# Moving the first weight load ahead of the entry barrier in a decode-attention kernel

## The chip, the cores and the metric

The kernel runs on one core of a Trainium2 chip. The metric is the device time of one execution in microseconds (us), median of several runs. Loads are issued by SyncE ("SP" in the profile, "SPq" for its queue). The 16 DMA engines of the core then move them.

## The reference

There are two independent attention decodes, A and B, with one query token each. D is 576, there are 32 query heads and 16 key/value heads of size 128. A sees a window of 2048 positions of the cache, B all 8192. The two results stand side by side in the output.

```python
q = (x @ wq).reshape(B, Sq, Hq, Dh)                       # x: 1 x 1 x 576, wq: 576 x 4096
scores = einsum("bhqd,bhkd->bhqk", q, k) * Dh ** -0.5     # k, v: the cache, repeated for 2 heads
o = einsum("bhqk,bhkd->bhqd", softmax(scores), v)
return o.reshape(B, Sq, Hq * Dh) @ wo                     # wo: 4096 x 576
```

With one token, nearly all the work is reading wq, the caches and wo once: 102.8 MB.

## The kernel before

The program is a list of operations per engine, with semaphores worked out from what each reads and writes. `emit` puts the lists into one block. The framework puts an entry barrier ahead of the block (each engine drains and reports to PoolE; PoolE releases all) and an exit barrier behind it.

```python
def load(dst, src, writes, dma, after=()):                # all big loads: SyncE
    add("sp", lambda sp: sp.dma_start(dst, src()), writes=writes, dma=dma, after=after)

def load_x(P):                                            # the two small x loads: ScalarE's queue
    def go(act):
        ...
            src = bass.AP(tensor=x.tensor, offset=x.offset, ap=[[9, 64], [4, 2], [1, 5]])
            return act.dma_start(xtwo[:, P, 0:5], src)    # 128 pieces of 5 elements, 10 bytes
    add("act", go, writes=[("xtwo", P)], dma="x%d" % P)
...
    with self.nc.Block() as block:                        # in emit
        @block.sync
        def _(sp):
            run("sp", sp)
        ...
...
prog.emit()
for P in range(2):                                        # behind the block and its exit barrier
    o = prog.writer[("out", P)]
    nc.sync.wait_ge(prog.sem(o.key), o.value)
```

The first nine loads of SyncE wait for nothing: six parts of wq (2 MB, 2 MB, 0.5 MB for A; the same for B) and three of the four first key slots. The tenth, into key slot 3, waits until PE is through with the part of wq that lies there.

## Time and profile before

| | before |
|---|---|
| time, median of 3 | 249.32 us (249.07 to 249.35) |
| span of the profiled run | 247.7 us |
| first packet of a load (packet records) | 1.74 us |
| last packet of wo ends (packet records) | 244.92 us |

The page's lines on the DMA. The first two rows have 40 slices of the span; a digit is the busy share in tenths. The last two give packets, MB and share of 16 engines' span per queue.

```profile
span 247.7 us, 7504 instructions
...
DMA  7999999999999999999999999999999999999993
GB/s 267 408 423 423 438 429 426 423 431 423 429 425 434 426 421 423 427 426 431 431 434 429 423 429 426 423 431 434 434 429 423 429 426 423 431 432 432 426 399 142
...
q1 hardware_dynamic: 7936, 102.77, 98.1%
...
q10 hardware_dynamic: 288, 0.00, 0.1%
```

The DMA engines are busy from the first slice to the last at some 425 GB/s. The Trainium skill ("DMA: Bandwidth & Descriptors", Specifications) puts the fabric ceiling at 435 GB/s; the inner slices (421 to 438) agree with that. So only the two ends have time to give: the head without a load, and the tail after the last one.

SyncE's waits (engine, line, releaser: us in total, times, longest) look as if SyncE were held by PE:

```profile
SPq L380 <- PE ktps L466: 87.5, 15, 16.4
SPq L380 <- PE opsum L557: 74.7, 14, 25.8
...
SPq L380 <- PE misc L425: 23.4, 1, 23.4
...
SPq L730 <- DMA out_dram<-outsb: 0.4, 1, 0.4
```

But loads land 18 to 31 us after issue: SyncE refills a queue that is never empty, and these waits cost nothing. Only the last line is at the end of the span.

The timeline of the first microsecond (start, duration, engine, line, operation):

```profile
0.34 0.10 POOL L743 MEMSET const-uint8-127<- 128x1 uint8 x1
0.73 0.20 POOL L353 MEMSET ident<- 128x128 bf16 x1 [0.29 <-POOLq L743]
0.74 0.61 ACTq L344 DMA_DIRECT2D xtwo<-in_A_x_dram  x1
0.74 0.86 SPq L380 DMA_DIRECT2D vslots<-in_A_wq_dram  x2
```

The issue of the first load, at 0.74, is in SyncE's power alone, yet stands behind a barrier that waits for PoolE's four memsets. What that head costs is seen in the view of windows (window and length, busy time of PE, PEld, DVE, ACT and POOL with counts, PE clock, DMA share, GB/s; a packet counts where it ends or starts, so short windows are rough):

```profile
0.00:1.00 1.00, 0.00 (x0) 0.00 (x0) 0.00 (x0) 0.00 (x0) 0.47 (x6) 1.00 0.00 0
1.00:2.00 1.00, 0.00 (x0) 0.00 (x0) 0.00 (x0) 0.00 (x0) 1.00 (x5) 1.00 1.14 229
2.00:3.00 1.00, 0.00 (x0) 0.00 (x0) 0.00 (x0) 0.97 (x1) 1.00 (x6) 1.00 0.29 98
3.00:4.00 1.00, 0.00 (x0) 0.00 (x0) 0.00 (x0) 0.52 (x2) 0.77 (x5) 1.00 1.01 426
```

And the tail, from the timeline:

```profile
245.39 0.11 PEld L646 LDWEIGHTS ktps<-vslots,opj 128*32 128x32 bf16 x4 [0.22 <-DMA vslots<-in_B_wo_dram]
245.75 0.31 DVE L652 CAST outsb<-ktps 128x144 bf16<-128x144 f32 x1 [10.44 <-PE ktps L646]
246.09 0.56 SPq L658 DMA_DIRECT2D out_dram<-outsb  x1
```

The output lands at 247.69 (the last increment of its semaphore; the prediction's 247.66 is the last but one), and SyncE's last wait ends the span at 247.74.

Drains and semaphore instructions are left out of the timeline; these are their records in the trace of the kernel before (start, ns, engine, operation):

```
  0.000     7 Sync    DRAIN             reports to PoolE
  0.304   188 GpSimd  DRAIN             behind its four memsets
  0.535    17 GpSimd  EVENT_SEMAPHORE   all four reported
  0.655    17 Sync    EVENT_SEMAPHORE   released
  0.740   386 Sync    DMA_DIRECT2D      first load
246.089   563 Sync    DMA_DIRECT2D      output
246.710   462 Sync    DRAIN             exit barrier
247.323    17 Sync    EVENT_SEMAPHORE   released
247.711    28 Sync    EVENT_SEMAPHORE   wait for the two output DMAs
```

### The profile page before, as it was taken

What the parts mean: (1) busy time and instruction counts of PE and PEld (TensorE: products, weight loads), DVE (VectorE), ACT (ScalarE), POOL (GpSimd) and SP (SyncE); (2) the same over time, 40 slices, a digit from 0 to 9 for tenths busy, and PEclk for the clock granted to TensorE, in tenths of its full rate; (3) what the DMA queues carried; (4) which work ended last, traced back from release to release, by engine and by line L of the source; (5) the groups of instructions that cost most, each with busy time, mean ns of one, the idle gap of its engine ahead of it and who ended that gap; (6) DMA issues with size and microseconds to landing.
All of it is one profiled execution on the core that took longest, in us unless ns stands there. A gap on an engine that the chain in (4) does not pass through costs nothing. (4 is left out here: it accounts for less than half of the span.)

```text
span 247.7 us, 7504 instructions
## 1 busy us (share of the span) xinstructions
PE 169.6 (68%) x3406; PEld 131.4 (53%) x3406; DVE 80.9 (33%) x152; ACT 87.1 (35%) x92; POOL 12.9 (5%) x49
## 2 busy tenths in 40 slices
PE   0193689984999569995999638998255144685634
PEld 0031277764787459783887428785243142584522
DVE  0001145663556025555656022555004004204000
ACT  2000057837478016786778004775200000000000
POOL 7501000000000000000000000000000000000000
PEclk9999779996799967999999956999858755556555
DMA  7999999999999999999999999999999999999993
GB/s 267 408 423 423 438 429 426 423 431 423 429 425 434 426 421 423 427 426 431 431 434 429 423 429 426 423 431 434 434 429 423 429 426 423 431 432 432 426 399 142
DMA packets 8235, 102.92 MB, mean 415 GB/s; under 512 B 1184, under 2 KB 1312, under 8 KB 2080
## 3 DMA queue, kind: packets, MB, share of 16 engines
q1 hardware_dynamic: 7936, 102.77, 98.1%
q8 instruction: 8, 0.13, 0.2%
q10 hardware_dynamic: 288, 0.00, 0.1%
q14 instruction: 3, 0.02, 0.0%
HBM read 102.76 MB, written 0.00 MB: 415 GB/s over the span
## 5 line engine op out<-in xcount | busy, mean ns | idle before, releaser
L472 ACT ACTIVATE kt<-ktps 128x1024 bf16<-128x1024 bf16 x80 | 77.8, 1021 | 52.8 <-PE ktps L466 52.8
L466 PEld LDWEIGHTS ktps<-ident,kslots 128*128 128x128 bf16 x1280 | 78.2, 103 | 27.1 <-issue 27.1
L466 PE MATMUL ktps<-ident,kslots 128*128 128x128 bf16 x1280 | 84.5, 229 | 11.1 <-PEq L214 11.1
L475 DVE COPY kt<-ktps 128x1024 bf16<-128x1024 bf16 x80 | 55.2, 691 | 52.5 <-PE ktps L466 52.4
L557 PE MATMUL opsum<-vslots,ptm 128*32 128x128 bf16 x1280 | 27.7, 259 | 28.4 <-PEq L214 24.6
L557 PEld LDWEIGHTS opsum<-vslots,ptm 128*32 128x32 bf16 x1280 | 24.8, 118 | 32.1 <-issue 32.0
L486 PE MATMUL sacc<-kt,qst 128*32 128x512 bf16 x320 | 25.5, 392 | 1.8 <-PEq L214 1.8
L566 DVE TENSOR_TENSOR diag<-opsum,rows 128x512 f32<-128x512 f32 x5 | 3.5, 692 | 55.8 <-PE opsum L557 55.8
L425 PE MATMUL opsum<-vslots,xpad 128*32 128x512 bf16 x64 | 8.4, 505 | 16.1 <-DVE xpad L410 12.2
L599 ACT ACTIVATE stat<-stat 128x1 f32<-128x1 f32 (+1 forms) x2 | 0.6, 295 | 37.4 <-DVE stat L597 37.4
L425 PEld LDWEIGHTS opsum<-vslots,xpad 128*32 128x32 bf16 x64 | 2.3, 118 | 19.0 <-issue 13.2
L457 POOL COPY qst<-qtm 128x64 bf16<-128x64 bf16 x20 | 4.5, 236 | 122.7 <-PE sacc L486 113.2
L646 PE MATMUL ktps<-kslots,opj 128*32 128x144 bf16 x184 | 6.1, 326 | 5.8 <-DMA kslots<-in_B_wo_dram 3.9
L431 ACT ACTIVATE qrow<-opsum 128x512 bf16<-128x512 f32 x2 | 1.2, 597 | 24.8 <-PE misc L425 24.8
L486 PEld LDWEIGHTS sacc<-kt,qst 128*32 128x32 bf16 x320 | 5.3, 94 | 8.4 <-issue 4.5
L523 ACT ACTIVATE psb<-sacc,stat 128x2048 bf16<-128x2048 f32 x3 | 5.9, 1967 | 8.5 <-DVE stat L517 8.5
L646 PEld LDWEIGHTS ktps<-kslots,opj 128*32 128x32 bf16 x184 | 5.2, 145 | 6.4 <-DMA kslots<-in_B_wo_dram 4.2
L425 PE MATMUL misc<-vslots,xpad 128*32 128x512 bf16 x64 | 8.3, 497 | 0.0
L433 DVE CAST qrow<-misc 128x512 bf16<-128x512 f32 x2 | 1.4, 691 | 16.3 <-PE misc L425 16.3
L630 PE MATMUL misc<-acc,pick 128*128 128x32 f32 x16 | 3.8, 404 | 3.6 <-DVE acc L624 2.9
L652 DVE CAST outsb<-ktps 128x144 bf16<-128x144 f32 x2 | 0.6, 308 | 16.3 <-PE ktps L646 16.3
L630 PEld LDWEIGHTS misc<-acc,pick 128*128 128x128 f32 x16 | 3.6, 328 | 3.8 <-DVE acc L624 3.0
(66 smaller groups left out, 63.1 us busy)
## 6 DMA issues: line engine op xcount, KB each, us to landing
kslots<-in_B_k_cache_dram SPq DMA_DIRECT2D x16, 2048.0 KB, 20.1
vslots<-in_B_v_cache_dram SPq DMA_DIRECT2D x16, 2048.0 KB, 18.3
kslots<-in_A_k_cache_dram SPq DMA_DIRECT2D x4, 2048.0 KB, 30.1
vslots<-in_A_v_cache_dram SPq DMA_DIRECT2D x4, 2048.0 KB, 25.1
vslots<-in_A_wq_dram SPq DMA_DIRECT2D x2, 2048.0 KB, 9.8
vslots<-in_B_wq_dram SPq DMA_DIRECT2D x2, 2048.0 KB, 20.3
kslots<-in_A_wo_dram SPq DMA_DIRECT2D x2, 2016.0 KB, 23.9
kslots<-in_B_wo_dram SPq DMA_DIRECT2D x1, 2016.0 KB, 31.2
```

The costliest lines, as they stand in the source:

```text
L425: ins = pe.matmul(qps[c][32 * j:32 * j + 32, :], lhsT=xpad[:, P, x, :], rhs=src[:, o:o + 512], start=(u == 0), stop=(u == WQ_UNITS - 1))
L433: add("dve", lambda dve: dve.tensor_copy(qrow[:, 512:1024], misc[:, :]), reads=[B_M], writes=[("qrow", 1)])
L457: add("pool", lambda pool: pool.tensor_copy(qst[:, s * 64:(s + 1) * 64], qtm[:, o:o + 64]), reads=[("qtm", KIND[g])], writes=[("qst", s)], ...
L466: ins = pe.matmul(ktps_bf[q][:, t * 128:(t + 1) * 128], lhsT=kslots[:, s, o:o + 128], rhs=ident[:, :], start=True, stop=True, is_transpose ...
L472: add("act", lambda act, q=q, dst=dst: act.activation(dst, ktps_bf[q], ACT.Copy), reads=[("bank", q)], writes=[("kt", u % NKT, q)], tag="e ...
L475: add("dve", lambda dve, q=q, dst=dst: dve.tensor_copy(dst, ktps_bf[q]), reads=[("bank", q)], writes=[("kt", u % NKT, q)], tag="e%d%d" % ( ...
L486: ins = pe.matmul(sacc[32 * j:32 * j + 32, 512 * half:512 * half + 512], lhsT=qst[:, s * 64 + e * 32:s * 64 + e * 32 + 32], rhs=rhs, start ...
L523: return act.activation(psb[:, :].rearrange("p (x g) -> p x g", g=2), src, ACT.Exp, bias=st(P, C_NB + k), scale=SCALE, accum_out=st(P, C_L ...
L557: ins = pe.matmul(opsum[32 * j:32 * j + 32, s * DH:(s + 1) * DH], lhsT=ptm[:, o:o + 32], rhs=vslots[:, s, b * 128:(b + 1) * 128], start=(u ...
L566: return dve.tensor_tensor(diag[:, g % 2, :, :], opsum[:, :].rearrange("p (s d) -> p d s", s=NS), m, ALU.mult)
L630: ins = pe.matmul(misc[:, 0:32], lhsT=pick[:, r, :], rhs=acc[:, d, 32 * r:32 * r + 32], start=(r == 0), stop=(r == 3))
L646: ins = pe.matmul(ktps[P][32 * j:32 * j + 32, 0:OUTW], lhsT=opj[:, P, jj:jj + 32], rhs=view[:, o:o + OUTW], start=(jj == 0), stop=(jj == H ...
```

## The change

Its description: the first load of wq precedes the entry barrier, and SyncE's wait for the two output DMAs stands behind the block's exit barrier. The intent is to start the loads while the other engines are still gathering, and to hide the exit barrier behind the landing of the output. The whole diff:

```diff
+        first = per["sp"].pop(0)
+        assert not first.left and first.dma is not None
+        one(self.nc.sync, first)
+        lead = self.nc.cur_bb.bb.instructions
+        ins = lead.pop()
+        at = next(k for k, o in enumerate(lead) if o.engine == ins.engine and "Drain" in str(o))
+        lead.insert(at, ins)
+
         with self.nc.Block() as block:
```

The load is emitted ahead of the block and then moved in front of SyncE's drain. It writes a buffer that nobody else touches yet. The diff says nothing of the output wait: that stands behind the exit barrier in both kernels.

## The prediction

> What bounds the kernel now: the load stream. The page's row of DMA shares is 9 in every slice but the first (7) and the last (3); the packets of the SyncE queue, 102.77 MB, take 98.1% of 16 engines' span, and between 1.9 and 242.9 us the trace never has fewer than 13 of them in flight. The stream moves 422 to 430 GB/s; the Trainium skill (DMA: Bandwidth & Descriptors, Specifications) gives 435 GB/s as the fabric ceiling, and the trace agrees that almost nothing is left. So the span is a head without loads (first packet at 1.74 us), 243.2 us of stream (the last packet of wo ends at 244.92) and a tail of 2.8 us (matmuls, one copy, output DMA issued at 246.09, landed at 247.66, end 247.74). SyncE waits for PE often (view of its queue's waits: 87 and 75 us), but loads land 18 to 31 us after issue and the queue never runs dry.
>
> What the change does. In the order of SyncE's instructions one load of 2 MB moves ahead of its drain into the entry barrier. Nothing else changes: the wait for the output DMAs stands behind the exit barrier in both kernels, so that half of the description is worth 0.
>
> Gain, from the timeline of the first 4 us: SyncE reaches its drain at 0.00, is released at 0.655 (PoolE, with four memsets and a drain, comes last, at 0.53), and issues the first load at 0.74; the issue takes 0.39, the first packet starts 0.62 us after its end (the same section's "~0.6 us" to the first byte agrees). Now the issue should start at about 0.00 and the first packet at 1.0: the stream starts 0.74 us earlier.
>
> Price: the drain now follows a DMA issue. At the kernel's end such a drain took 0.46 us. So SyncE joins at about 0.9, the barrier releases at 1.05, and the other engines (x loads, PoolE's setup) start 0.4 us later. The second load is issued at about 1.15 (before: 1.19), while the first keeps the engines busy for 5 us (8 packets of 0.62 each): no hole. The 0.4 us is hidden: the first matmuls start at 11.5 us, and the first load that waits for them, issued at 29.4, comes some 7 us (estimate: 15.3 MB queued ahead at 427 GB/s) before the queue would run dry.
>
> So 0.74 us lies on the critical path, once, and should appear at the end nearly in full. Span 247.7 -> 247.0 us; time 249.32 -> 248.6 us, range 248.1 to 249.2; that is 0.3%. Faster by over 2%: 0.005; within 2%: 0.985; slower by over 2%: 0.01.
>
> Right if: first issue at about 0.0, first packet at 1.0; barrier release 0.3 to 0.5 us later; second issue at 1.1 to 1.2; no gap in the loads in flight; last wo packet near 244.2; tail unchanged at 2.8; x landing at most 1 us later, without consequence.
>
> Wrong if: the drain lasts until the load's descriptors are written or the load has landed (5 us), which would hold all engines; or the queue is not ready so early and the first packet does not move; or the stream's rate varies between executions by as much as the gain (0.3% of it is 0.74 us), so that the time shows nothing.

## The result, and the profile after

The changed kernel took 248.41 us, median of 4 (248.08 to 248.61), the kernel before 249.23 us in the same rounds. The ratio is 0.9966, 95% interval 0.9949 to 0.9984: a real gain of some 0.8 us, far under 2%. A second time with five rounds, as an experiment below, it was 0.9973.

The page, timeline and windows after, in the same order as before:

```profile
span 247.2 us, 7504 instructions
...
DMA  8999999999999999999999999999999999999993
GB/s 316 382 446 420 436 424 424 427 427 435 427 426 424 424 432 422 426 424 427 430 432 430 430 424 438 424 427 424 430 427 432 427 432 430 432 425 423 422 410 143
```

```profile
0.00 1.14 SPq L388 DMA_DIRECT2D vslots<-in_A_wq_dram  x2
...
0.33 0.10 POOL L751 MEMSET const-uint8-127<- 128x1 uint8 x1
0.80 0.20 POOL L361 MEMSET ident<- 128x128 bf16 x1 [0.36 <-POOLq L751]
0.81 0.61 ACTq L352 DMA_DIRECT2D xtwo<-in_A_x_dram  x1
```

```profile
0.00:1.00 1.00, 0.00 (x0) 0.00 (x0) 0.00 (x0) 0.00 (x0) 0.41 (x6) 1.00 0.00 0
1.00:2.00 1.00, 0.00 (x0) 0.00 (x0) 0.00 (x0) 0.00 (x0) 1.00 (x4) 1.00 1.18 262
2.00:3.00 1.00, 0.00 (x0) 0.00 (x0) 0.00 (x0) 0.90 (x1) 1.00 (x5) 1.00 0.96 393
```

The issue moved from 0.74 to 0.00, and the first packet (packet records) from 1.74 to 1.02. From 2 to 3 us the stream already moves 393 GB/s, where the kernel before moved 98 GB/s in that window. The other four engines started only 0.07 us later. (The two issues of the first timeline line are merged: the second load was issued at 0.805.) The tail has kept its shape:

```profile
245.18 0.31 DVE L660 CAST outsb<-ktps 128x144 bf16<-128x144 f32 x1 [10.22 <-PE ktps L654]
245.51 0.56 SPq L666 DMA_DIRECT2D out_dram<-outsb  x1
```

From the last wo packet (244.35) to the end (247.17) are 2.82 us, and 2.81 before.

To see whether the gain is kept, I summed the bytes of the load packets in order of time and read from both traces when each amount had been moved. The difference is the lead over the kernel before, in us:

| profile | at 1 MB | 2 MB | 4 MB | 10 MB | 50 MB | 102 MB |
|---|---|---|---|---|---|---|
| changed kernel | 0.73 | 0.67 | 0.55 | 0.58 | 0.54 | 0.54 |
| changed kernel, again | 0.62 | 0.63 | 0.78 | 0.72 | 0.72 | 0.73 |

In the columns from 4 MB on the lead stays within 0.04 and 0.06 us, and read at every 0.05 MB in between within 0.14, for 230 us. Whatever PE and SyncE do in between neither eats nor adds to it. Within the first 4 MB it wanders by 0.1 to 0.2 us from one execution to the next. In the first profile the stream had a dip where the second load took over (10 to 12 packets in flight, not 16, from 6.7 to 6.9 us). In the second profile it had none. The last 0.8 MB, which the table leaves out, shift the lead once more from run to run, by -0.19 to +0.37 us over all profiles of this document: at the last packet of wo it is 0.58 and 0.90 us in these two. So a single span shows the gain only to within some 0.2 to 0.4 us; the tables and the medians carry it.

### The profile page after: what moved, and what is told of

Its sections match the earlier page's. It is cut to its first block, busy times and chain, and to the rows that moved or that the text cites. A ratio compares the mean times of both kernels' runs of the same rounds, so it can differ in the third digit from the quotient of the medians.

```text
span 247.2 us, 7504 instructions
## 1 busy us (share of the span) xinstructions
PE 169.9 (69%) x3406; PEld 132.4 (54%) x3406; DVE 80.9 (33%) x152; ACT 87.2 (35%) x92; POOL 12.9 (5%) x49
## 5 line engine op out<-in xcount | busy, mean ns | idle before, releaser
L474 PEld LDWEIGHTS ktps<-ident,kslots 128*128 128x128 bf16 x1280 | 79.3, 104 | 26.2 <-issue 26.2
L474 PE MATMUL ktps<-ident,kslots 128*128 128x128 bf16 x1280 | 85.6, 230 | 10.7 <-PEq L214 10.7
```

Source lines behind the costliest of these rows:

```text
L474: ins = pe.matmul(ktps_bf[q][:, t * 128:(t + 1) * 128], lhsT=kslots[:, s, o:o + 128], rhs=ident[:, :], start=True, stop=True, is_transpose ...
```

## The experiments

Theory A: the kernel is a stream of loads with two ends, and the time follows the moment of the first packet one to one. Rivals: the difference is chance (B); compute paces the kernel and the head hides in slack (C); the start of the other engines counts (D); the amount loaded ahead counts (H). The place of the output wait is a question by itself.

### The changed kernel again

No edit; five rounds.

> The changed kernel again, for a second profile and a tighter interval. Theory A (only the start of the load stream counts): first packet at 1.02 us, the last wo packet 0.5 to 0.75 us earlier than before, ratio 0.9970 (0.9960 to 0.9980), that is 0.55 to 0.9 us. The dip of the stream at 6.7 us (where the second load takes over, and where the first profile lost 0.18 of its 0.73 us of lead) is seen again if it belongs to the change, and is gone if it was chance. Theory B (the difference is chance between executions): ratio within 0.999 to 1.001.

Measured: 248.36 us, ratio 0.9973 (0.996 to 0.9987), first packet at 1.05, last wo packet at 244.02, no dip. B falls, A holds. One figure missed: the last wo packet came 0.90 us earlier, not 0.5 to 0.75; the last 0.8 MB added 0.18 to the lead of 0.73. The dip is not part of the change.

### The first load later

```diff
+        reads = ["ones"] if dma == "wq00" else []          # wait for PoolE's memsets
-        add("sp", lambda sp: sp.dma_start(dst, src()), writes=writes, dma=dma, after=after)
+        add("sp", lambda sp: sp.dma_start(dst, src()), reads=reads, writes=writes, dma=dma, after=after)
```

> The kernel before, with its first load made to wait until PoolE's memsets are done, so that the issue moves from 0.74 to about 3.75 us; every other engine starts as before. Theory A (each us of the stream's start is a us of the time): first packet at 4.75, time 252.2 us (ratio 1.012, from +2.9 to +3.1 us). Rival C (the kernel is paced by what the engines compute, and a start of the loads hides in the slack that keeps SyncE waiting for PE): at most +0.5 us, ratio below 1.002.

Measured: 251.68 us (249.02 before), ratio 1.0099 (1.0084 to 1.0115). This is the timeline of SyncE and, below it, the last two windows of the first 10 us:

```profile
3.68 0.86 SPq L381 DMA_DIRECT2D vslots<-in_A_wq_dram  x2
```

```profile
3.00:4.00 1.00, 0.00 (x0) 0.00 (x0) 0.00 (x0) 0.52 (x2) 0.77 (x5) 1.00 0.03 1
4.00:10.00 6.00, 0.00 (x0) 0.00 (x0) 0.71 (x3) 0.00 (x0) 4.71 (x14) 1.00 0.88 330
```

The first packet came at 4.70, 2.95 us later than before, and the time grew by 2.5 to 2.7 us. C falls. But my figure of 2.9 to 3.1 was missed too. The lead table says where: -3.02 us at 1 MB, -2.70 at 4 MB, and -2.65 at 102 MB. Some 0.37 us were won back, 0.3 of it between 2 and 4 MB, and kept. In this run the 288 small packets of the x loads moved between 2.1 and 3.2 us, before the stream began. In the other kernels they stand among the big ones (4.8 to 13.3 us in the changed kernel). That made a new theory, X: the small packets cost the stream about 0.3 us. It is tested below.

### All nine wait-free loads ahead

```diff
-        first = per["sp"].pop(0)
+        while not per["sp"][0].left:                       # until a load has to wait
+            ... one(...) and move it ahead of SyncE's drain, as in the change ...
```

> The changed kernel with all nine wait-free loads ahead of the drain, not one. SyncE takes about 5.5 us to issue them, so the other four engines pass the barrier at about 5.8 us, 5 us later than in the changed kernel. Theory A (the stream's first packet counts, and the engines' start hides in their slack of some 7 us): first packet at 1.02 us, time as that of the changed kernel, 248.4 us, ratio 0.9970 within 0.001; if the dip at 6.7 us came from what the other engines do then (the x loads), it is gone and the ratio is 0.9960. Rival D (the start of the other engines counts): +3 to +5 us, ratio 1.010 to 1.020.

Measured: 248.28 us, ratio 0.9971 (0.9958 to 0.9985). The timeline shows the other engines 4.8 us late:

```profile
2.95 1.95 SPq L387 DMA_DIRECT2D kslots<-in_A_k_cache_dram  x3
5.55 0.20 POOL L360 MEMSET ident<- 128x128 bf16 x1 [5.11 <-POOLq L750]
5.56 0.61 ACTq L351 DMA_DIRECT2D xtwo<-in_A_x_dram  x1
```

PE's first wait (waits of the engines, us in total, times, longest), in order for the kernel before, the changed kernel and this one:

```profile
PE opsum L425 <- DVE xpad L410: 12.2, 2, 11.5
```

```profile
PE opsum L433 <- DVE xpad L418: 12.7, 2, 12.0
```

```profile
PE opsum L432 <- DVE xpad L417: 14.7, 2, 14.0
```

PE starts 2 us later than in the changed kernel and the time is the same: D falls. With nine loads ahead, none of them depends on the barrier any more, and the time shows no more gain. In the one profile the lead at 102 MB is 0.83 us, a little above the 0.54 and 0.73 of the changed kernel; the times of five runs each (248.28 and 248.36 in the median) do not tell the two apart.

### One small piece ahead, cut along the rows

```diff
+            for p0, p1, r, name in ((0, 16, ("v0", "part"), "wq00a"), (16, 128, res, "wq00")):
+                load(dst[p0:p1, :], ... rows p0:p1 ..., [r], name)      # the first piece goes ahead
```

> The changed kernel with only 16 of the 128 rows of the first load (one packet of 16 KB per DMA engine) ahead of the drain, the other 112 behind the barrier. Theory A (what counts is when the first packet moves, as long as the second load is issued before the first one is through): first packet at 1.0 us (a little sooner if the issue of 16 rows is shorter than 0.39 us), the second load issued at 0.8 and its packets from 1.8 on, while the first packets (1.1 to 1.5 us each) are still moving: ratio 0.9972, as the changed kernel. Rival H (the amount ahead counts): half or less of the gain, ratio 0.9985 or more.

Measured: 251.46 us, ratio 1.0099 (1.0084 to 1.0115), some 2.4 us slower than the kernel before. Neither theory had said that. The first packet came at 1.03 as expected, but afterwards the stream ran at 70% of its rate, as the window from 4 to 10 us shows, first in the changed kernel, then in this one:

```profile
4.00:10.00 6.00, 0.00 (x0) 0.00 (x0) 0.29 (x1) 0.00 (x0) 4.71 (x14) 1.00 0.98 396
4.00:10.00 6.00, 0.00 (x0) 0.00 (x0) 0.29 (x1) 0.00 (x0) 4.71 (x14) 1.00 1.02 279
```

The engines are busy, but packets of 16 KB take 0.8 to 1.1 us (medians of 16 in order of time) from 3.8 to 10.5 us, against 0.61 in the changed kernel. The slow stretch ends as the load of the 112 rows lands (its semaphore rises from 10.2 to 11.0 us). So this run tried the shape of the pieces, not the amount ahead. The next two runs separate the two.

### The same cut with nothing ahead, and another cut

The kernel before with the same cut into 16 and 112 rows, both behind the barrier:

> The kernel before, nothing ahead of the barrier, with its first load cut along the rows into 16 and 112. If the loss of the cut along the rows is all the shape of the pieces (Theory S), it appears here too, as large: 3.1 us over the kernel before, 252.2 us, ratio 1.0125, with packets of 0.8 to 1.1 us in the first 10 us. If it came from having a small piece ahead of the barrier (Rival H), this kernel is as the kernel before, ratio 1.000 to 1.002.

Measured: 252.39 us, ratio 1.0138 (1.0122 to 1.0153), 3.3 us slower, with packets of 0.8 to 1.1 us in the same stretch and a lead of -3.10 us at 4 MB that stays (-3.19 at 102 MB). The cut alone does it. The Trainium skill ("SBUF — State Buffer", Door 1: The DMA port swizzle) says that DMA bandwidth depends on how many of the 16 SBUF ports the partitions reach. By its mapping, 16 neighbouring rows reach four of them. But most of the slow packets are those of the other 112 rows, which by the same mapping reach all 16. So the count of ports alone does not explain the loss, no run here shows the ports, and the cause is open.

The changed kernel with the first load cut along the columns, so that each packet goes to the rows it went to before:

```diff
+            for c0, c1, r, name in ((0, 1024, ("v0", "part"), "wq00a"), (1024, n * WQ_U, res, "wq00")):
+                load(dst[:, c0:c1], ... columns c0:c1 ..., [r], name)   # 128 x 2 KB ahead, 128 x 14 KB behind
```

> The changed kernel with one eighth of the first load ahead of the drain, cut along the columns this time: 128 rows of 2 KB ahead, 128 rows of 14 KB behind the barrier, so that every packet goes where it went before. The cut along the rows (16 and 112) lost 3.1 us against the changed kernel, but the trace shows its packets of 16 KB in the first 10 us at 0.8 to 1.1 us each, against 0.61, so it tried the shape of the pieces and not how much is ahead. Theory A (only the time of the first packet counts, as long as the second load takes over in time): first packet at 1.0 us; the second load is issued at 0.80 and its packets come at 1.8; one hole of at most 0.3 us where the eighth is through before that: ratio 0.9972 to 0.9985. Rival H (the amount ahead counts): ratio 0.999 or more.

Measured: 248.54 us, ratio 0.9979 (0.9966 to 0.9993), first packet at 1.00. The lead is 0.61 us at 0.5 MB, 0.44 at 2 MB and 0.48 at 102 MB. An eighth of the load ahead keeps two thirds or more of the lead. What is lost is lost at the handover: the small packets are through at about 2.1 us, and the first packets of the second piece, from there, are slow again (up to 1.16 us for 14 KB, against 0.54 later; that this is the whole loss is argued, not shown). The ratio lies in A's range and excludes 1; against H's 0.999, the top of the interval falls just short of excluding it, and the lead decides: most of the gain comes with an eighth of the bytes.

### The x loads

Without x (zeros in its place, so the result is wrong):

> The changed kernel without the two x loads (x is set to zero instead, so the result is wrong on purpose). The run with the late load gained back 0.37 us of its 3.02 us between 2 and 4 MB; there the 288 small packets of x had been moved before the stream began. Theory X (each small packet of x that stands between the large ones costs the stream time, some 0.3 us in all): the lead of the stream over the kernel before grows from about 0.65 at 1 MB to about 1.0 at 10 MB, ratio 0.9960. Rival Y (that was chance; small packets are free): lead at 10 MB 0.55 to 0.75, ratio 0.9972.

Measured: 247.89 us, ratio 0.9951 (0.9937 to 0.9965). (Its comparison with the reference passed all the same. In a simulation of both programs with these inputs its output differs from that of the kernel before by 0.2% in norm: the scores are so small that the attention weights hardly depend on x.)

With x as one row of 1152 bytes per load, spread by engines that idle there anyway:

```diff
-    xtwo = nc.alloc_sbuf_tensor("xtwo", [128, 2, 8], BF16)
+    xrow = nc.alloc_sbuf_tensor("xrow", [1, 2, DM], BF16)
+    xexp = nc.alloc_sbuf_tensor("xexp", [1, 2, 5, 128], BF16)
-            return act.dma_start(xtwo[:, P, 0:5], src)
+            return act.dma_start(xrow[0:1, P, :], xs[P][0, 0:1, :])
+        # VectorE: xexp[0, P, j, 2m + e] = xrow[0, P, 9m + 4e + j], one copy
+        # PE, for j in 0..4: matmul(ktps[P][:, j:j+1], lhsT=xexp[0:1, P, j, :], rhs=ident[0:1, 0:1])
+        # then as before, from ktps[P][:, 0:5] in place of xtwo[:, P, 0:5]
```

> The changed kernel with x loaded as one row of 1152 bytes per DMA and spread over the partitions by one VectorE copy and five 1-column matmuls each, so that some 32 small packets are left of 256. Right result expected. Theory X: ratio 0.9960 to 0.9965, lead at 10 MB about 0.95. Rival Y: ratio 0.9972, as the changed kernel. The first matmuls may start earlier or later than 11 us; that should not matter.

Measured: 248.07 us, ratio 0.9958 (0.9945 to 0.9972), and the comparison with the reference passed. As a zero x passes it too, I looked further: in simulation, this kernel and the next give the output of the kernel before bit for bit, with these inputs and with x 300 times as large, where a zero x is 2 to 3% off. The page's line of ScalarE's queue, 288 packets in the kernel before (256 of 10 bytes, 32 of 4 bytes), is now

```profile
q10 hardware_dynamic: 4, 0.00, 0.0%
```

| profile | at 1 MB | 2 MB | 4 MB | 10 MB | 102 MB |
|---|---|---|---|---|---|
| changed kernel, twice | 0.73, 0.62 | 0.67, 0.63 | 0.55, 0.78 | 0.58, 0.72 | 0.54, 0.73 |
| without x | 0.76 | 0.77 | 1.07 | 1.13 | 1.12 |
| x as rows | 0.68 | 0.70 | 1.00 | 1.07 | 1.05 |
| nine loads ahead | 0.67 | 0.70 | 0.97 | 0.95 | 0.83 |
| nine loads ahead, x as rows (below) | 0.76 | 0.77 | 1.06 | 1.22 | 1.08 |

Without the small packets the lead grows by some 0.4 us between 2 and 10 MB, and stays. X holds, with a little more than its 0.3 us. The leads decide it: the interval of x as rows (0.9945 to 0.9972) overlaps that of the changed kernel. With nine loads ahead the small packets come later (9.5 to 16.5 us) and cost less, 1.08 against 0.83 at the end, so 0.25 us, from one profile each. The Trainium skill says that DMAs of different issuing engines run on the same 16 DMA engines and interleave ("DMA: Bandwidth & Descriptors", Issuing engines are not separate DMA queues), and that under 512 bytes a DMA engine does a read-modify-write (Specifications). The first agrees with the records. The records do not show the second: the small packets are listed with 9 ns each, 0.16 us per DMA engine in sum, less than half of what they cost. (I had guessed 32 packets for the row form. It was 4, since each row went in one piece.)

Both good moves together, nine loads ahead and x as rows:

> Both moves that were as fast or faster than the changed kernel: nine loads ahead of the drain, and x loaded as one row. Theory X: the small packets are gone and nothing else is on the path, so the time is that of the kernel with x as one row, 248.07 us, ratio 0.9955 to 0.9965. If the nine loads hid some of their own gain behind the x packets (they landed late, and the lead fell by 0.12 us where they came), it gets 0.1 us more.

Measured: 247.89 us, result as above, ratio 0.9955 (0.9942 to 0.9969), lead 1.08 us at 102 MB. Its five runs (247.82 to 247.97) lie below all nine of the changed kernel (248.08 to 248.83). Those ran in other rounds, five of them on another chip, but the kernel before took much the same there (medians 249.02 and 249.23 against 249.07). It beats both kernels. Against x as rows alone (247.90 to 248.32) the difference is within what the intervals leave open.

### The output wait inside the block

```diff
             def _(sp):
                 run("sp", sp)
+                for P in range(2):
+                    o = self.writer[("out", P)]
+                    sp.wait_ge(self.sem(o.key), o.value)
```

The two waits behind `prog.emit()` are taken away. First in the changed kernel:

> The changed kernel with SyncE's wait for the two output DMAs moved ahead of the exit barrier. My theory: the exit barrier (drain and gather, release, seen to take 0.08 to 0.6 us) hides behind the landing of the output, which came 0.33 us after the barrier's release; moved inside, the barrier comes after the landing and costs its own length, so the span ends about 0.3 us later than in the changed kernel (tail from the output's issue to the end 1.95 us and not 1.63), ratio to the kernel before 0.998. Rival: the wait's place is worth nothing, tail 1.63 us, ratio 0.997; or it is worth as much as the early load, 0.7 us, and the time is that of the kernel before.

Measured: 249.28 us, ratio 1.0007 (0.9994 to 1.0021): 0.9 us slower than the changed kernel in the same rounds, three times what I expected. The last of the rivals came true: the wait's place is worth about as much as the early load. SyncE's waits of the two, the changed kernel first:

```profile
SPq L738 <- DMA out_dram<-outsb: 0.4, 1, 0.4
```

```profile
SPq L262 <- DMA out_dram<-outsb: 1.0, 1, 1.0
```

The records say why. In the changed kernel the output lands at 247.12, and the span ends at 247.17, since the exit barrier has run meanwhile. With the wait inside, it lands at 247.31, and then come two waits, a drain and the barrier, to 247.77. That is 0.46 us after the landing, not 0.04, so 0.42 of the 0.9. Most of the rest is outside the span: the time measured less the span of the same run is 1.81 us, and 1.44 in the first profile of the changed kernel. To test that, the same move in the kernel before:

> The kernel before with SyncE's wait for the two output DMAs moved ahead of the exit barrier, without the early load. The earlier run of the same move in the changed kernel cost 0.9 us, of which its profile showed 0.42 us between the landing of the output and the end of the span, and 0.35 us in the time outside the span (1.81 us against 1.44 to 1.53 of all others). Theory F (the place of the wait is worth 0.4 us within the span, and more outside it because all engines now leave together at the end): ratio 1.0035 (+0.7 to +1.0 us), landing to end about 0.50 us, outside 1.75 to 1.85 us. Rival G (the place is worth only what the span shows, the rest of the 0.9 was chance): +0.4 us, ratio 1.0017, outside 1.45 to 1.53.

Measured: 249.8 us, ratio 1.0027 (1.0013 to 1.004), so 0.7 us. From landing to end are 0.46 us, and outside the span are 1.80 us. (The 0.50 that was expected is 0.03 longer because it counts from the last increment but one.) The ratio fell a little short of F's figure, and its interval holds G's 1.0017 too; but both parts are as F said, and G's 1.45 to 1.53 outside is out. The eleven profiles with the wait behind the barrier have 1.44 to 1.55 outside, the two with the wait inside 1.80 and 1.81. All runs whose spans are on record agree: 1.75 to 1.94 in the ten with the wait inside, 1.39 to 1.56 in the others. That all engines, not SyncE alone, still have to finish then is my explanation, and it is only argued.

## Why the prediction was right or wrong

- **The load stream bounds the kernel: right.** Shifts of its start came out at its end, in both directions; in every profile that I compared the lead stayed within 0.15 us between 15 and 102 MB. The last 0.8 MB added up to 0.37 us of their own.
- **0.74 us gained, once, and kept: right in kind and size.** 0.72 and 0.70 us at the first packet, 0.54 and 0.73 at 102 MB, 0.8 and 0.7 us in the time. Predicted was 248.6 us in 248.1 to 249.2; measured were 248.41 and 248.36.
- **The first packet 1.0 us after the issue starts: right** (1.02). The distance from the issue's end, 0.62 before and 0.63 after, agrees with the 0.6 us to the first byte of the skill's page ("DMA: Bandwidth & Descriptors", Specifications), which does not say from where it counts.
- **The price was mis-sized.** The step was "At the kernel's end such a drain took 0.46 us. So SyncE joins at about 0.9, the barrier releases at 1.05, and the other engines start 0.4 us later". The drain behind the first load took 0.124 us, SyncE was released at 0.720 (0.655 before) and the other engines started 0.07 us later. The drain behind nine loads took 0.37. So the length of a drain behind one DMA does not carry over to another. What sets it is open. It made no difference, as nine loads ahead showed: even 4.8 us on the other engines cost nothing.
- **The second load at 1.15 us: wrong for the same reason** (0.805), and harmless. No hole in the stream: right on average. One of the two profiles had a short dip.
- **The output wait worth 0: right for this diff**, which leaves it where it was. As a design it is worth 0.7 to 0.9 us, as much as the early load.
- **The slack of 7 us: not measured as such.** A start 4.8 us later, and 2 us later for PE's first matmul, fits in it. The bound itself was not tried. (The nine loads are 15.7 MB, not 15.3, so the same estimate gives some 8 us.)
- **Not seen: the small packets of x.** The prediction took the stream's rate as fixed. They cost about 0.4 us in the changed kernel, about half of what the change gained.

## What to carry to other kernels

This is one kernel, and the advice goes as far as its runs. In a kernel that streams loads as this one does, at some 425 GB/s, look at the two ends and at foreign packets: when the first packet moves, what runs after the last one, and which small transfers stand among the big ones. Wait-free loads can go ahead of the entry barrier, and one is enough, if it lasts until the next one arrives. When a piece is to be cut smaller, try the columns before the rows (the cut into 16 and 112 rows lost some 3 us, that into columns at most 0.25 us of lead), and look at the time of its packets. A final wait that only one engine needs belongs behind the exit barrier: 0.7 to 0.9 us here.

## What the Trainium skill lacked or had wrong

- "DMA: Bandwidth & Descriptors": what packets of 10 and 4 bytes cost a running stream of large ones. 288 of them cost about 0.4 us here (0.25 us with nine loads ahead), while their own records add up to 0.16 us per DMA engine.
- "DMA: Bandwidth & Descriptors", Where 436 GB/s comes from, says that for transfers between HBM and SBUF the HBM side, some 358 GB/s, binds. It did not here: with one core running, this kernel loaded some 425 GB/s from HBM all along, and the fabric's 435 GB/s fitted. (Under Measured, the page itself ties the 358 to both cores of a pair streaming, and has 425 GB/s for one core.)
- "DMA: Bandwidth & Descriptors": the size of the loss from cutting one load of 128 rows into 16 and 112 (packets of 0.8 to 1.1 us instead of 0.61; 3.1 to 3.3 us in the time). "SBUF — State Buffer" has the port mapping, but not this case.
- "DMA: Bandwidth & Descriptors": the first 16 packets of a load of 16 KB packets onto idle engines took 1.1 to 1.3 us each (medians of the twelve profiles that start so) instead of 0.61. No line there tells it.
- No page: how long a drain behind a DMA issue lasts. It took 0.12 us behind the first load, 0.37 behind nine, 0.46 behind the output.
- No page ("Runtime: NRT & Kernel Launch" is the nearest): the time outside the span depends on how the kernel ends, 1.44 to 1.55 us in the profiled runs where SyncE's wait stood behind the exit barrier, 1.80 and 1.81 us where it stood inside.
